# A fused attention and dense kernel: the ordering model's times, held loads, the early output by PE transposes and the band added in PSUM are changed together

## The chip, the cores and the metric

The kernel runs on one core of one Trainium2 chip. The metric is the device time of one execution in microseconds (us); smaller is better. Most executions of a kernel lie within a few us of each other. A run at a lower granted TensorE clock, or over 1.5% above the fastest of its kernel, counts as slow and stays out of the comparisons. Kernels are compared through their ratio to the kernel before, measured in the same rounds.

Names of engines: PE is TensorE, DVE is VectorE, ACT is ScalarE, POOL is GpSimd, SP issues DMAs. A line number such as L626 is a line of the kernel in question, so the same piece of code has different numbers in different kernels.

## The reference, cut to what matters

```python
# q, k, v: 8 batches x 8 heads x 576 tokens x 64
q_d, k_d, v_d = mean over groups of 4 tokens            # 144 pooled tokens
out_up    = repeat(softmax(q_d @ k_d.T / 8) @ v_d, 4)    # pooled attention, each row for 4 tokens
mask      = abs(i - j) < 4                               # a band
out_local = softmax(where(mask, q @ k.T / 8, -1e9)) @ v
x = (out_up + out_local) as [4608 tokens, 512]
h = x @ w_in                                             # [4608, 2048]
return (h - tanh(h)) @ w_out                             # [4608, 512]
```

## The kernel before: the parts that matter

The program is recorded first and ordered afterwards. Every operation is put down with an engine, a duration in ns, the tiles it reads and writes, and its PSUM banks. A list scheduler then runs through a model of the five engines and the DMA queue, decides the order (and, where `choice` offers several engines, which of them does the work), and the instructions are issued in that order. At run time each engine takes its instructions strictly in line. A wrong duration gives no wrong result; it gives an order that makes an engine wait behind something that is late.

```python
class Program:
    LAT = {"PE": 270, "ACT": 150, "DVE": 110, "POOL": 150, "SP": 50, "DMA": 2200}
    ...
    def op(self, eng, ns, fn, reads=(), writes=(), pri=0, slack=0, fill=(), drain=()): ...
    def choice(self, alternatives, ...): ...
    def dma(self, eng, ns, fn, cost, piece, src=(), dst=(), ...): ...
    def order(self): ...        # the list scheduler
```

There are 32 pairs of heads, four for each batch. Dense work on 512 tokens may start when the pairs of their batches have written `xT`. All but the first four pairs run beside dense matmuls. One pair, cut:

```python
        # p >= 12: qr transposed by DMA, then put in place by ACT; before that, PE transposes
        if p >= T_DMA:
            P.dma("SP", 1740, lambda: nc.sync.dma_start_transpose(
                out=qT[s], in_=qr[s].rearrange("p a c -> p (a c)")), 1300, 72, ...)
            op("ACT", 1250, lambda: A.copy(...), reads=[("qT", s)], writes=[("qk", s, 0), ("qk", s, 5)])
        # ... scores s1 and s2 on PE into PSUM t1, t2; then exp, then (p >= 4) the band as a product
        op("ACT", 960, lambda: A.activation(out=e1, in_=two(t1)[:, :, 0:480], func=AF.Exp, scale=SCALE),
           drain=[t1], writes=[("E", e, 0)], pri=pri)
        if p >= NP:
            op("DVE", 950, lambda: V.tensor_tensor(
                out=e1, in0=e1,
                in1=mask[:, 0:480].unsqueeze(1).to_broadcast([128, 2, 480]),
                op=ALU.mult), reads=["mask"], writes=[("E", e, 0)], pri=pri)
        # ... the same for e2v; value product `outs` on PE; reciprocal and ln on DVE
        def back():              # p < 12: out of ln into xT's layout, pooled rows expanded 4 times
            for half in range(2):
                T.matmul(two(tb)[:, half, 0:288], ln[s][:, 5, :], up[:, 288 * half:288 * half + 288],
                         start=True, stop=False)
            T.matmul(two(tb)[:, 1, 224:288], ln[s][0:16, 6, :], up[0:16, 0:64], start=False, stop=False)
            for t in range(NT):
                ...              # 6 matmuls against the identity, added in the same banks
        if p >= X_DMA:           # p >= 12: DMA transpose of ln, then the join
            P.dma("SP", 1350, lambda: nc.sync.dma_start_transpose(...), 1000, 72, ...)
            P.choice([("DVE", 1900, lambda: join(V)), ("POOL", 1400, lambda: join(GP))],
                     reads=[("lT", s)], writes=[("x", b, j)], pri=pri)
            return
        op("PE", 450 * cold, back, ...)
        P.choice([("DVE", 720, lambda: V.tensor_copy(out=xs, in_=two(tb)[:, :, 0:288])), ("ACT", 680, ...)], ...)
```

And a dense block: `mm1` (four matmuls into one bank, tanh on ACT into `u`, subtraction on DVE into `gT`) and `mm2` (sixteen matmuls into one bank, copy on ACT into `y`, store).

The softmax here doesn't subtract the row's maximum and nothing guards it: scores larger than these inputs give would overflow.

Of the kernel before, what the change touches and what calls it, by code (L numbers as in the profile page):

```python
# [9 lines left out]
BF16 = mybir.dt.bfloat16  # L10
AF = mybir.ActivationFunctionType
ALU = mybir.AluOpType
# [11 lines left out]
class Program:  # L24

    LAT = {"PE": 270, "ACT": 150, "DVE": 110, "POOL": 150, "SP": 50, "DMA": 2200}
    RING = 230

    def __init__(self):
        self.ops = []  # L30
        self.alternatives = {}
        self.slack = []
        self.soon = set()
        self.goal = set()
        self.ring = {}
        self.rings = {}
        self.touch = []
        self.use = []
        self.toks = []
        self.cap = {}  # L40
        self.last_write = {}
        self.readers = {}
# [66 lines left out]
    def order(self):  # L109
# [56 lines left out]
        for i in range(n):  # L166
            if left[i] == 0:
                make_ready(i)
        for step in range(n):
            best = None  # L170
            for eng, cand in ready.items():
                if not cand:
                    continue
                now = max(free.get(eng, 0.0), min(at[i] for i in cand))
                if eng == "PE":
# [5 lines left out]
                elif eng == "DMA":  # L181
                    pick = min((turn.get(self.ring[i][0], -1), start[self.ring[i][1]], i)
                               for i in cand if at[i] <= now)[2]
                else:
                    pick = min((self.ops[i][4], i) for i in cand if at[i] <= now)[1]
# [12 lines left out]
            end = now + self.ops[i][1]  # L198
            want = [t for t in self.use[i] if t.first == i]
# [57 lines left out]
def kernel(  # L257
# [41 lines left out]
    mask = fixed("mask", [128, 576], BF16)  # L299
# [19 lines left out]
    up = lT[1].rearrange("p n c -> p (n c)")[:, 0:S]  # L319
    r = fixed("r", [128, 2, 7], FP32, 2)  # L320
    ln = fixed("ln", [128, 7, 128], BF16, 2)
# [31 lines left out]
    def c_up():  # L353

        GP.memset(up, 1.0)
        GP.affine_select(out=up, in_=up, compare_op=ALU.is_ge, fill=0.0,
                         base=0, pattern=[[1, S]], channel_multiplier=-4)
        GP.affine_select(out=up, in_=up, compare_op=ALU.is_ge, fill=0.0,
                         base=3, pattern=[[-1, S]], channel_multiplier=4)

# [8 lines left out]
    def c_mask():  # L369

        GP.memset(mask, 1.0)
        m4 = mask[:, 0:480].rearrange("p (t c) -> p t c", c=QW)
        for part, pat in ((m4, [[0, 4], [1, QW]]),
                          (mask[:, 480:576], [[1, 96]])):
            neg = [[-s, n] for s, n in pat]
            GP.affine_select(
                out=part, in_=part, compare_op=ALU.is_ge, fill=0.0,
                base=-1, pattern=neg, channel_multiplier=1)
            GP.affine_select(
                out=part, in_=part, compare_op=ALU.is_ge, fill=0.0,  # L380
                base=7, pattern=pat, channel_multiplier=-1)
        GP.affine_select(
            out=mask[:, 0:QW], in_=mask[:, 0:QW], compare_op=ALU.is_ge,
            fill=0.0, base=-4, pattern=[[0, QW]], channel_multiplier=1)
        GP.affine_select(
            out=mask[:, 480:576], in_=mask[:, 480:576], compare_op=ALU.is_ge,
            fill=0.0, base=99, pattern=[[0, 96]], channel_multiplier=-1)
# [6 lines left out]
    def load_qk(p):  # L394

        b, h0, s = p // NP, 2 * (p % NP), p % NQKN
        for i, src in enumerate((q, k)):
# [6 lines left out]
            load(600, issue, [("qkn", s, i)], T_QK, 380, -30, 8, (), eng)  # L404

    def load_v(p):
# [3 lines left out]
        for i in range(2):  # L410
# [21 lines left out]
            load(620, issue, [("vst", s, i)], T_V, 100, -30, 40)  # L432
# [24 lines left out]
    def load_v4(p):  # L457
# [8 lines left out]
        load(520, issue, [("v4", s)], 900, 184, -30, 18)  # L466

    def pool_v4(p):
# [9 lines left out]
        op("POOL", 1150, a1, reads=[("v4", s)], writes=["v2"], pri=10 * p - 12)  # L478
        op("POOL", 750, a2, reads=["v2"], writes=[("vp", s)], pri=10 * p - 12)

    def pool_v(hb):
# [15 lines left out]
        op("ACT", 590, lambda: A.copy(  # L497
# [5 lines left out]
    def attention(p):  # L503
# [10 lines left out]
        if p >= NEARLY:  # L514
            op("POOL", 1300, lambda: GP.tensor_copy(  # L515
# [14 lines left out]
        if p >= T_DMA:  # L530
            P.dma("SP", 1740, lambda: nc.sync.dma_start_transpose(
                out=qT[s], in_=qr[s].rearrange("p a c -> p (a c)")), 1300, 72,
                  src=[("qr", s, 0), ("qr", s, 1)], dst=[("qT", s)], pri=-50, lead=500)
            op("ACT", 1250, lambda: A.copy(  # L534
# [3 lines left out]
        else:  # L538
            for a0, a1, tn, cn in ((0, 5, 290, 740), (5, 9, 230, 620)):
# [10 lines left out]
                def copy(fn, a0=a0, a1=a1, b16=b16):  # L550
# [5 lines left out]
                          ("DVE", cn, lambda copy=copy: copy(V.tensor_copy))][:1 + (p < NP)],  # L556
# [10 lines left out]
        def add2(eng):  # L567
            with nc.allow_low_precision("pooled q and k"):
                eng.tensor_tensor(out=qkd[s][:, 0:G],  # L569
                                  in0=half[:, :, 0, :],  # L570
                                  in1=half[:, :, 1, :], op=ALU.add)
        P.choice([(name, n1, lambda eng=eng: add1(eng)) for name, n1, _, eng in adders],
# [41 lines left out]
        if new:  # L614
            op("PE", 620, s12, slack=late, reads=qks + [("qkd", s)], fill=[t1, t2], pri=pri)
        else:
            op("PE", 420 * cold + 250 * (p < NP), s1, slack=late,
               reads=qks + ["bias"] * (p < NP), fill=[t1], pri=pri)
# [3 lines left out]
        op("ACT", 960, lambda: A.activation(  # L622
            out=e1, in_=two(t1)[:, :, 0:480], func=AF.Exp, scale=SCALE),
           drain=[t1], writes=[("E", e, 0)], pri=pri)
        if p >= NP:
            op("DVE", 950, lambda: V.tensor_tensor(  # L626
                out=e1, in0=e1,
                in1=mask[:, 0:480].unsqueeze(1).to_broadcast([128, 2, 480]),
                op=ALU.mult), reads=["mask"], writes=[("E", e, 0)], pri=pri)
        yield  # L630
        if not new:
            op("PE", 380 * cold + 100 * (p < NP), s2, slack=late, reads=qks + [("qkd", s)],
               fill=[t2], pri=pri)
        op("ACT", 310, lambda: A.activation(  # L634
            out=e2v, in_=two(t2)[:, :, 0:96], func=AF.Exp, scale=SCALE),
           drain=[t2], writes=[("E", e, 1)], pri=pri)
        op("ACT", 650, lambda: A.activation(  # L637
            out=e3, in_=two(t2)[:, :, 96:384], func=AF.Exp, scale=SCALE / 16.0),
           drain=[t2], writes=[("E", e, 2)], pri=pri)
        if p >= NP:  # L640
            op("DVE", 450, lambda: V.tensor_tensor(  # L641
                out=e2v, in0=e2v,
                in1=mask[:, 480:576].unsqueeze(1).to_broadcast([128, 2, 96]),
                op=ALU.mult), reads=["mask"], writes=[("E", e, 1)], pri=pri)
# [25 lines left out]
        op("DVE", 200, lambda: V.reciprocal(out=r[s], in_=blocks()[:, :, :, 64]),  # L670
           drain=[to], writes=[("r", s)], pri=pri)
        op("DVE", 1060, lambda: V.tensor_tensor(  # L672
# [6 lines left out]
        tb = P.psum(2, kind)  # L679

        def back():
            for half in range(2):
                T.matmul(two(tb)[:, half, 0:288], ln[s][:, 5, :], up[:, 288 * half:288 * half + 288],
                         start=True, stop=False)
            T.matmul(two(tb)[:, 1, 224:288], ln[s][0:16, 6, :], up[0:16, 0:64],
                     start=False, stop=False)
            for t in range(NT):
                q0, q1 = QW * t, QW * t + NQ[t]
                for half in range(2):
                    c0, c1 = max(q0, 288 * half), min(q1, 288 * half + 288)  # L690
                    if c0 < c1:
                        T.matmul(two(tb)[:, half, c0 - 288 * half:c1 - 288 * half],  # L692
                                 ln[s][0:NQ[t], t, :], ident[0:NQ[t], c0 - q0:c1 - q0],
                                 start=False, stop=(t == (2, NT - 1)[half]))
        if p >= X_DMA:
            P.dma("SP", 1350, lambda: nc.sync.dma_start_transpose(
                out=lT[s], in_=ln[s].rearrange("p n c -> p (n c)")), 1000, 72,
# [3 lines left out]
            def join(eng):  # L701
# [12 lines left out]
            P.choice([("DVE", 1900, lambda: join(V)), ("POOL", 1400, lambda: join(GP))],  # L714
                     reads=[("lT", s)], writes=[("x", b, j)], pri=pri)
            return
        op("PE", 450 * cold, back, slack=late, reads=[("ln", s), ("lT", 1), "ident"],
           fill=[tb], pri=pri)
        xs = xT[j][:, b * S:(b + 1) * S].rearrange("p (n c) -> p n c", n=2)
        P.choice([("DVE", 720, lambda: V.tensor_copy(out=xs, in_=two(tb)[:, :, 0:288])),  # L720
                  ("ACT", 680, lambda: A.copy(out=xs, in_=two(tb)[:, :, 0:288]))],
                 drain=[tb], writes=[("x", b, j)], pri=pri)
# [4 lines left out]
    def mm1(kb, fc):  # L727
# [14 lines left out]
        op("ACT", 590, lambda: A.activation(  # L742
            out=u[us], in_=one(tok), func=AF.Tanh),
           drain=[tok], writes=[("u", us)], pri=DPRI)
        op("DVE", 670, lambda: V.tensor_tensor(  # L745
# [6 lines left out]
    def mm2(kb, i):  # L752
        ts, part, g = i // 4, i % 4, kb % 2
        if part == 0:
            ycur[0] = P.psum(1, "d")
        tok = ycur[0]

        def mm(e):
            for fc in range(4 * part + 2 * e, 4 * part + 2 * e + 2):
                T.matmul(one(tok), gT[g][:, fc, ts * 128:ts * 128 + 128],  # L760
                         w_out_sb[:, fc, :],
                         start=(fc == 0), stop=(fc == N_FF - 1))
        for e in range(2):
            op("PE", 432, lambda e=e: mm(e),
               reads=[("w_out", part, c) for c in range(4)] +
               [("gT", g, fc) for fc in range(4 * part, 4 * part + 4)],
               fill=[tok], pri=5000)
        if part == 3:
            ys = yn[0] % 3
            yn[0] += 1  # L770
            op("ACT", 590, lambda: A.copy(out=y[ys], in_=one(tok)),  # L771
               drain=[tok], writes=[("y", ys)], pri=DPRI)
            r0 = kb * 512 + ts * 128
            P.dma("SP", 530, lambda: nc.sync.dma_start(
                out=out[r0:r0 + 128, :], in_=y[ys]), 700, 344, src=[("y", ys)], pri=DPRI)

    def dense(kb):
# [13 lines left out]
        for i in range(16):  # L791
            if kb < NBLK:
# [4 lines left out]
    M2_FIRST, T_DMA, X_DMA, NEW, LATE = 16, 12, 12, 12, 0  # L797
    DPRI = -1
    T_QK, T_V, T_W, W_PRI, NEARLY = 800, 1000, 2850, 32, NP
    CAST_V = [[("POOL", 820, GP.tensor_copy), ("ACT", 640, A.copy)],  # L800
              [("POOL", 820, GP.tensor_copy)]]
    any3 = [("DVE", 700, V.tensor_copy), ("ACT", 650, A.copy),
            ("POOL", 750, GP.tensor_copy)]
# [141 lines left out]
```

## Time and profile before

| | before |
|---|---|
| time, 3 runs | 336.77 us median (335.35 to 337.07) |
| profiled execution | 331.7 us, span 329.7 us, granted clock 1.0 |
| first dense matmul (head) | 25.4 us |
| from there to the end of the last matmul (stretch) | 299.9 us |
| after the last matmul (tail) | 4.4 us |

The page of the kernel before, its parts 1 and 2: busy us, share of the span and instructions of each engine; and the busy share of the DMA engines in 40 slices of the span, in tenths:

```profile
PE 314.8 (95%) x2420; PEld 158.8 (48%) x2461; DVE 214.0 (65%) x330; ACT 202.4 (61%) x334; POOL 177.3 (54%) x211
DMA  7999999999999999999999999972320011000121
```

PE is busy nearly always, so PE's list of work and PE's waits decide. DMA is full until about 214 us, so what arrives when is decided by the order of the queue.

The engines' busy time between 120 and 185 us, kernel before. After the length of the stretch come busy us (and instructions) of PE, weight loads, DVE, ACT and POOL, the granted clock, the DMA share and GB/s:

```profile
120.00:185.00 65.00, 61.26 (x514) 30.79 (x521) 57.14 (x73) 44.82 (x72) 57.05 (x62) 1.00 1.11 246
```

DVE and POOL are at 88% of this stretch, and PE, which should be the limit, is at 94%.

Whom PE waited for, kernel before: us in total, number of waits, the longest:

```profile
PE bank L650 <- DVE E L641: 2.0, 2, 1.4
...
PE bank L650 <- DVE E L626: 0.5, 1, 0.5
PE bank L650 <- DVE gT L745: 0.4, 1, 0.4
```

L650 is the value product; L626 and L641 are the two mask products. The groups of DVE instructions show why those are late. After the bar come busy us and the mean ns of one, then the idle time before them:

```profile
L672 DVE TENSOR_TENSOR ln<-bank,r 128x896 bf16<-128x896 f32 x32 | 34.7, 1087 | 0.9
L626 DVE TENSOR_TENSOR E<-E,mask 128x960 bf16<-128x960 bf16 x28 | 32.3, 1154 | 11.5 <-ACT E L622 11.4
L641 DVE TENSOR_TENSOR E<-E,mask 128x192 bf16<-128x192 bf16 x28 | 16.1, 576 | 0.7 <-ACT E L634 0.7
L703 DVE TENSOR_TENSOR xT<-lT 128x480 bf16<-128x480 bf16 x9 | 12.3, 1366 | 1.4 <-DMA lT<-ln 1.4
```

The means hide a spread. L626 takes 0.641 us at best, 0.896 in the median, 3.479 at worst; L672, which reads PSUM, stays between 1.027 and 1.093.

```profile
124.79 0.67 POOL L569 TENSOR_TENSOR qkd<-half 128x288 bf16<-128x288 f32 x1
125.43 1.00 POOL L703 TENSOR_TENSOR xT<-lT 128x480 bf16<-128x480 bf16 x1
126.40 0.34 POOL L709 TENSOR_TENSOR xT<-lT 128x96 bf16<-128x96 bf16 x1
126.69 1.14 POOL L515 CAST qr<-qkn 128x1152 bf16<-128x1152 f32 x1
```

The multiply, which takes 0.64 us at best, ended only 0.5 us after four POOL instructions that followed each other without a gap.

### The profile page before, as it was taken

What the parts mean: (1) busy time and instruction counts of PE and PEld (TensorE: products, weight loads), DVE (VectorE), ACT (ScalarE), POOL (GpSimd) and SP (SyncE); (2) the same over time, 40 slices, a digit from 0 to 9 for tenths busy, and PEclk for the clock granted to TensorE, in tenths of its full rate; (3) what the DMA queues carried; (4) which work ended last, traced back from release to release, by engine and by line L of the source; (5) the groups of instructions that cost most, each with busy time, mean ns of one, the idle gap of its engine ahead of it and who ended that gap; (6) DMA issues with size and microseconds to landing.
All of it is one profiled execution on the core that took longest, in us unless ns stands there. A gap on an engine that the chain in (4) does not pass through costs nothing.

```text
span 329.7 us, 6505 instructions
## 1 busy us (share of the span) xinstructions
PE 314.8 (95%) x2420; PEld 158.8 (48%) x2461; DVE 214.0 (65%) x330; ACT 202.4 (61%) x334; POOL 177.3 (54%) x211
## 2 busy tenths in 40 slices
PE   7989999999999999999899899999999999999994
PEld 2654555665444544444444445444444444444441
DVE  4767864479966969888989869757754433444300
ACT  4968864588778866687867375868543444344311
POOL 8664547959667698869899848787310000000000
PEclk9999999999999999999999999999999999999999
DMA  7999999999999999999999999972320011000121
GB/s 233 288 235 228 241 229 218 316 278 234 284 224 254 226 208 264 252 253 269 206 257 247 251 238 276 212 172 61 91 60 34 32 52 45 32 32 32 43 86 65
DMA packets 108862, 59.80 MB, mean 181 GB/s; under 512 B 86174, under 2 KB 96030, under 8 KB 108830
## 3 DMA queue, kind: packets, MB, share of 16 engines
q1 hardware_dynamic: 104318, 54.60, 71.0%
q0 software_dynamic: 4224, 4.19, 7.7%
q10 hardware_dynamic: 288, 0.59, 0.6%
q8 instruction: 19, 0.31, 0.4%
q14 instruction: 13, 0.11, 0.1%
HBM read 43.64 MB, written 9.44 MB: 161 GB/s over the span
## 4 chain that ended last, share of the span: by engine, by line
PE 76%; DVE 12%; DMA 3%; ACT 3%; POOL 2%; issue 2%; ACTq 0%; DVEq 0%; POOLq 0%
PE bank L760 32%; PE bank L734 32%; DMA lT<-ln 3%; DVE E L626 3%; PE bank L650 3%; PE bank L584 3%; DVE ln L672 3%; DVE gT L745 2%; PE bank L657 2%; DVE E L641 2%; DVE xT L709 1%; ACT E L622 1%; PE bank L692 1%; DVE xT L703 1%; PE bank L547 1%
## 5 line engine op out<-in xcount | busy, mean ns | idle before, releaser
L734 PE MATMUL bank<-xT,w_in_sb 128*128 128x512 bf16 x557 | 143.7, 379 | 1.4 <-DVE gT L745 0.3
L760 PE MATMUL bank<-w_out_sb,gT 128*128 128x512 bf16 x555 | 141.6, 379 | 1.5 <-issue 0.6
L745 DVE TENSOR_TENSOR gT<-bank,u 128x512 bf16<-128x512 f32 x144 | 97.3, 685 | 61.4 <-ACT u L742 60.9
L742 ACT ACTIVATE u<-bank 128x512 f32<-128x512 f32 x144 | 86.0, 598 | 76.7 <-PE bank L734 73.6
L760 PEld LDWEIGHTS <-gT 128*128 128x128 bf16 x576 | 53.9, 98 | 62.0
L734 PEld LDWEIGHTS <-w_in_sb 128*128 128x128 bf16 x576 | 53.9, 98 | 61.9 <-issue 0.5
L564 POOL TENSOR_TENSOR half<-qk 128x576 f32<-128x576 bf16 x28 | 32.1, 1146 | 20.7 <-ACT qk L551 12.3
L626 DVE TENSOR_TENSOR E<-E,mask 128x960 bf16<-128x960 bf16 x28 | 32.3, 1154 | 11.5 <-ACT E L622 11.4
L622 ACT ACTIVATE E<-bank 128x960 bf16<-128x960 f32 x32 | 31.2, 974 | 12.3 <-PE bank L584 12.2
L515 POOL CAST qr<-qkn 128x1152 bf16<-128x1152 f32 x28 | 32.7, 1169 | 8.0 <-DMA qT<-qr 5.5
L672 DVE TENSOR_TENSOR ln<-bank,r 128x896 bf16<-128x896 f32 x32 | 34.7, 1087 | 0.9
L771 ACT COPY y<-bank 128x512 f32<-128x512 f32 x36 | 21.1, 586 | 19.7 <-PE bank L760 18.3
L451 POOL CAST vw<-vst 128x640 bf16<-128x640 f32 x31 | 25.4, 824 | 7.5 <-DMA vst<-in_v_dram 7.5
L472 POOL TENSOR_TENSOR v<-v 72x512 f32<-72x512 f32 x20 | 25.4, 1272 | 1.2 <-DMA v<-in_v_dram 0.4
L534 ACT COPY qk<-qT 128x1152 bf16<-128x1152 bf16 x20 | 24.1, 1205 | 0.6 <-DMA qT<-qr 0.6
L650 PE MATMUL bank<-vw,E 128*128 128x65 bf16 x320 | 20.1, 194 | 3.1 <-DVE E L641 2.0
L569 POOL TENSOR_TENSOR qkd<-half 128x288 bf16<-128x288 f32 x29 | 21.0, 725 | 1.7 <-DVE r L670 0.8
L476 POOL TENSOR_TENSOR vp<-v 72x256 bf16<-72x256 f32 x20 | 14.6, 730 | 13.1 <-PE bank L657 13.0
L650 PEld LDWEIGHTS <-E 128*128 128x128 bf16 x320 | 16.5, 98 | 10.2 <-DVE E L641 2.5
L637 ACT ACTIVATE E<-bank 128x576 bf16<-128x576 f32 x32 | 21.1, 660 | 0.0
L703 POOL TENSOR_TENSOR xT<-lT 128x480 bf16<-128x480 bf16 x11 | 11.2, 1017 | 14.4 <-DMA lT<-ln 14.3
L641 DVE TENSOR_TENSOR E<-E,mask 128x192 bf16<-128x192 bf16 x28 | 16.1, 576 | 0.7 <-ACT E L634 0.7
(75 smaller groups left out, 225.7 us busy)
## 6 DMA issues: line engine op xcount, KB each, us to landing
vst<-in_v_dram SPq DMA_DIRECT2D x62, 160.0 KB, 5.2
qkn<-in_q_dram SPq DMA_DIRECT2D x32, 288.0 KB, 5.4
out_dram<-y SPq DMA_DIRECT2D x36, 256.0 KB, 4.7
qkn<-in_k_dram SPq DMA_DIRECT2D x30, 288.0 KB, 5.7
v<-in_v_dram SPq DMA_DIRECT2D x20, 288.0 KB
w_in_sb<-in_moe_w_in_dram POOLq DMA_DIRECT2D x4, 512.0 KB, 11.7
w_out_sb<-in_moe_w_out_dram POOLq DMA_DIRECT2D x4, 512.0 KB, 10.3
qkn<-in_k_dram ACTq DMA_DIRECT2D x2, 288.0 KB, 3.3
```

The costliest lines, as they stand in the source:

```text
L451: P.choice([(eng, ns, lambda fn=fn: fn(out=vw[w][:, 2 * jj:2 * jj + 2, :, 0:64], in_=vst[s])) for eng, ns, fn in CAST_V[p >= NEARLY]], rea ...
L472: GP.tensor_tensor(out=v2, in0=v4[s][:, :, :, 0:128], in1=v4[s][:, :, :, 128:256], op=ALU.add)
L515: op("POOL", 1300, lambda: GP.tensor_copy(out=qr[s].rearrange("p a (h d) -> p h a d", h=2), in_=qkn[sn].rearrange("p h (a d) -> p h a d", ...
L564: eng.tensor_tensor(out=half, in0=four[:, :, 0:2, :], in1=four[:, :, 2:4, :], op=ALU.add)
L622: op("ACT", 960, lambda: A.activation(out=e1, in_=two(t1)[:, :, 0:480], func=AF.Exp, scale=SCALE), drain=[t1], writes=[("E", e, 0)], pri=pri)
L626: op("DVE", 950, lambda: V.tensor_tensor(out=e1, in0=e1, in1=mask[:, 0:480].unsqueeze(1).to_broadcast([128, 2, 480]), op=ALU.mult), reads= ...
L650: T.matmul(two(to)[:, hh, 65 * t:65 * t + 65], E[e][:, c:c + 128], vw[w][:, 2 * jj + hh, t, :], start=True, stop=True)
L672: op("DVE", 1060, lambda: V.tensor_tensor(out=ln[s].rearrange("p n (h d) -> p h n d", d=D), in0=blocks()[:, :, :, 0:64], in1=r[s].unsqueez ...
L734: T.matmul(one(tok), w_in_sb[:, dc, fc * 128:(fc + 1) * 128], xT[dc][:, kb * 512:kb * 512 + 512], start=(dc == 0), stop=(dc == N_DC - 1))
L742: op("ACT", 590, lambda: A.activation(out=u[us], in_=one(tok), func=AF.Tanh), drain=[tok], writes=[("u", us)], pri=DPRI)
L745: op("DVE", 670, lambda: V.tensor_tensor(out=gT[g][:, fc, :], in0=one(tok), in1=u[us], op=ALU.subtract), drain=[tok], reads=[("u", us)], w ...
L760: T.matmul(one(tok), gT[g][:, fc, ts * 128:ts * 128 + 128], w_out_sb[:, fc, :], start=(fc == 0), stop=(fc == N_FF - 1))
```

## The change: its intent, and the diff

Four things are changed together.

1. The ordering model gets longer DMA times (a transpose of q and k 1684 instead of 1300 ns, of the output 1317 instead of 1000), shorter engine times, a rule for DVE and POOL additions that exclude each other, and `mm2` banks of its own. From pair 17 on, loads of q and k wait for the DMA transpose of the pair five before.
2. Work is placed differently: joins on POOL only, v casts also on ACT, scores as one block from pair 8 (before: 12), the last 128 output rows in two halves.
3. The output of the first 12 pairs goes through seven PE transposes into one bank; the pooled rows are added by DVE.
4. The band is added in PSUM, as -32768, before exp, instead of multiplied after exp.

The diff, cut (`...` marks cuts; changes of a mere duration are left out except a few):

```diff
-    LAT = {"PE": 270, "ACT": 150, "DVE": 110, "POOL": 150, "SP": 50, "DMA": 2200}
+    LAT = {"PE": 235, "ACT": 145, "DVE": 110, "POOL": 140, "SP": 50, "DMA": 2000}
...
+            if eng == "POOL" or eng == "DVE" and i in self.port:
+                port = end
...
-            P.dma("SP", 1740, lambda: nc.sync.dma_start_transpose(
-                out=qT[s], in_=qr[s].rearrange("p a c -> p (a c)")), 1300, 72,
+            P.dma("SP", 1340, lambda: nc.sync.dma_start_transpose(
+                out=qT[s], in_=qr[s].rearrange("p a c -> p (a c)")), 1684, 92,
...
-        if new:
-            op("PE", 620, s12, ...)
+        if p >= MERGE:
+            op("PE", 590, s12, ...)
...
+        def band(tok, lo, hi):
+            part = two(tok)[:, :, 0:hi - lo]
+            V.tensor_tensor(out=part, in0=part, in1=bias[:, lo:hi].unsqueeze(1)
+                            .to_broadcast([128, 2, hi - lo]), op=ALU.add)
+        if p >= NP:
+            op("DVE", 1080, lambda: band(t1, 0, 480), reads=["bias"], fill=[t1], pri=pri)
         op("ACT", ..., lambda: A.activation(out=e1, in_=two(t1)[:, :, 0:480], func=AF.Exp, scale=SCALE), ...)
-        if p >= NP:
-            op("DVE", 950, lambda: V.tensor_tensor(out=e1, in0=e1, in1=mask[:, 0:480]..., op=ALU.mult), ...)
...
-        tb = P.psum(2, kind)
+        tb = P.psum(1, kind)
         def back():
-            for half in range(2):
-                T.matmul(two(tb)[:, half, 0:288], ln[s][:, 5, :], up[:, 288 * half:288 * half + 288], ...)
-            ...
+            for t in range(7):
+                q0, n = (QW * t, NQ[t]) if t < NT else (S + 128 * (t - NT), (128, 16)[t - NT])
+                T.transpose(flat()[:, q0:q0 + n], ln[s][0:n, t, :], ident[0:n, 0:n])
...
-            P.choice([("DVE", 1900, lambda: join(V)), ("POOL", 1400, lambda: join(GP))],
+            P.choice([("POOL", 1310, lambda: join(GP))],
...
+        P.choice([("DVE", 130, lambda: V.tensor_copy(out=od[s], in_=flat()[:, S:S + G])), ("ACT", 170, ...)], ...)
+        op("DVE", 610, lambda: V.tensor_tensor(
+            out=xT[j][...], in0=flat()[:, 0:S]..., in1=od[s].unsqueeze(2).to_broadcast([128, G, 4]), op=ALU.add), ...)
...
+        split = kb == NBLK - 1 and ts == 3      # the last output rows: two banks of 256 columns
...
-    CAST_V = [[("POOL", 820, GP.tensor_copy), ("ACT", 640, A.copy)],
-              [("POOL", 820, GP.tensor_copy)]]
+    CAST_V = [[("POOL", 770, GP.tensor_copy), ("ACT", 620, A.copy)],
+              [("POOL", 770, GP.tensor_copy), ("ACT", 620, A.copy)]]
...
-            load_qk(nl[0])
+            t = nl[0] - BACK                    # BACK = 5
+            load_qk(nl[0], [("qT", t % 2)] if t >= T_DMA else ())
...
-    P.cap = {"b": 6, "d": 4}
+    P.cap = {"b": 6, "d": 4, "y": 3}
```

## The prediction

> **What bounds the kernel now.** TensorE. The busy table gives PE 314.8 of 329.7 us (95%), VectorE 65%, ScalarE 61%, GpSimd 54%; PEclk is full throughout. The chain of waits has three parts. (1) A head of 25.4 us until the first dense matmul (L734): an attention prologue over all engines, with mask, ident, group and expansion matrix made in turn on POOL, and a last pair whose loads land at about 13 us. (2) A PE stretch from 25.4 to 325.3 us: 1152 dense matmuls at a pitch of 0.216 us are 249 us, so attention's matmuls, changes of operand and stalls take some 51 us. (3) A tail of 4.4 us: y copy (0.59 us), then the store.
> The timeline shows true PE stalls of about 4.5 us in part 2. The largest (0.66, 0.61, 0.82, 1.4 us, between 127 and 184 us) are in the value product (L650), waiting for VectorE: mask multiply L641 or a late gT. The mask multiply (L626) takes 0.64 us at best, 1.15 on average, 3.48 at worst. The Trainium skill, "SBUF — State Buffer", section "SBUF: two separate sides", says a VectorE operation with two SBUF inputs and a GpSimd operation reading SBUF exclude each other for the whole instruction; this spread agrees, while PSUM readers (L672: 1.03 to 1.09 us) hardly vary.
>
> **What the change does, costed.**
> - Output by PE transposes for the first 12 pairs: L683+L685+L692 cost 0.85 us of PE a pair inside the dense stretch (6.8 us for 8). Seven transposes at the 0.056 us pitch of L547 are 0.4 us. Critical: -3.4 us.
> - Scores issued as one block for pairs 8 to 11: -0.8 us of PE.
> - Band added in PSUM before exp: two VectorE operations of, estimated from L745 and L672, 1.1 and 0.3 us, nearly constant, instead of 1.15 and 0.58 with long outliers. The value product then waits for ScalarE only. All joins go to POOL (9 x 2.26 us leave VectorE, 9 x 1.48 us reach POOL); 19 v casts leave POOL for ScalarE. Of 4.5 us of stalls I expect 3 to go.
> - Longer DMA times and loads held back: DMA share is above 1.0 from 25 to 185 us, so the bytes get no cheaper; only transposes should wait less. A guard against new stalls.
> - Head: the expansion matrix (1.9 us of POOL) and the bias operation go, ident comes first. But pairs 2 and 3 wait for loads, and the output gets a copy plus an add on VectorE. -0.6 us.
> - Tail: last output in two halves, smaller copy and store: -0.5 us.
>
> Sum -8.3 us; I give 1 us back for new waits, since PSUM is held longer by the band add and x now comes from POOL alone.
>
> **Prediction.** 329.2 us from 336.77 (-2.2%), range 326 to 333.5. Faster by over 2%: 0.56; within 2%: 0.42; slower: 0.02.
>
> **What would show it.** Output transposes near 0.43 us a pair on PE; first dense matmul at 24.5 to 25.2 us; the band add near 1.1 us with little spread, VectorE busy from 214 to about 185 us; no wait of L650 on VectorE's mask; POOL about 175 us; PE stalls in the dense stretch under 2 us; tail under 4.1 us. Wrong if PE stalls do not shrink, or the dense start does not move.
>
> **What would make it wrong.** The order is fixed in advance: if DMA transposes land later than planned, PE waits in line at scores (L584), or dense blocks wait for POOL's xT. If the head is bound only by loads, its gain vanishes and the result stays just within 2%. If the stalls vanish entirely and the head shrinks by 2 us, it goes to 326.

## More of the kernel before

The worst L626, in the order of time of DVE and then of POOL (start us, length us):

```profile
124.86 3.48 DVE L626 TENSOR_TENSOR E<-E,mask 128x960 bf16<-128x960 bf16 x1
```

## The result, and the profile after

| | before | after |
|---|---|---|
| time, 4 runs each | 336.21 us median (335.35 to 337.07) | 326.65 us median (325.31 to 327.17) |
| ratio | | 0.971, 95% interval 0.967 to 0.975: faster |
| profiled execution | 331.7 us, span 329.7 us | 327.17 us, span 325.3 us |
| head, stretch, tail | 25.4, 299.9, 4.4 us | 25.0, 296.8, 3.4 us |

A ratio is, to within 0.001, the mean time of one kernel's fast runs over that of the other's of the same rounds, so it is not quite the ratio of the medians.

The two traces differ by 4.4 us (head -0.4, stretch -3.1, tail -0.9), the timed runs by 9.6 us. The trace of before is of a quick execution: of the 53 other timed runs of before (without one slow profiled run) only one was below 331.7 us. So part of the timed gain is not seen in the traces.

The page after, the same lines:

```profile
PE 311.2 (96%) x2410; PEld 159.9 (49%) x2450; DVE 193.4 (59%) x322; ACT 207.4 (64%) x353; POOL 168.4 (52%) x209
DMA  7999999799974999999999999999711300000021
```

DVE lost 21 us. DMA has a gap between about 90 and 106 us (its share between 98 and 106 us is 0.49), where loads are held back; u_dma below, which holds none back, has no such gap. The windows view after, 120 to 185 us:

```profile
120.00:185.00 65.00, 64.29 (x494) 32.08 (x501) 40.70 (x64) 46.73 (x78) 46.26 (x54) 1.00 1.09 246
```

DVE fell from 57.1 to 40.7 us in this stretch, POOL from 57.1 to 46.3, and PE rose to 99%. The groups after, of the band and the join:

```profile
L626 DVE TENSOR_TENSOR bank<-bank,bias 128x960 f32<-128x960 f32 x28 | 32.4, 1159 | 19.3 <-PE bank L586 16.2 <-ACT vw L452 3.1
L626 DVE TENSOR_TENSOR bank<-bank,bias 128x192 f32<-128x192 f32 x28 | 10.0, 356 | 1.9 <-PE bank L608 1.9
L696 POOL TENSOR_TENSOR xT<-lT 128x480 bf16<-128x480 bf16 x20 | 20.2, 1009 | 16.4 <-DMA lT<-ln 16.4
```

The large band addition is no quicker on average than the product was (1.159 against 1.154 us), but its slowest is 1.167 us. Whom PE waited for after:

```profile
PE bank L764 <- DMA w_out_sb<-in_moe_w_out_dram: 2.0, 1, 2.0
...
PE bank L731 <- DVE gT L742: 0.7, 1, 0.7
```

The waits for the mask are gone and a new one has come: 2.0 us for the last quarter of `w_out`. In sum, PE's waits in the stretch (those over 0.15 us) were 4.3 us before and are 4.2 us after, so in these two traces they hardly shrank. The stretch is shorter because the rest of it, PE's work and its smaller steps, fell from 295.6 to 292.6 us. In order of time on PE after (start us, length us; x is the number of matmuls merged in the line), both the transposes and the wait:

```profile
55.31 0.59 PE L687 MATMUL bank<-ident,ln 120*128 120x120 bf16 x7
55.84 0.40 PE L548 MATMUL bank<-ident,qr 128*128 128x128 bf16 x4
56.07 1.46 PE L764 MATMUL bank<-w_out_sb,gT 128*128 128x512 bf16 x6
57.37 0.59 PE L687 MATMUL bank<-ident,ln 120*128 120x120 bf16 x7
59.98 0.38 PE L764 MATMUL bank<-w_out_sb,gT 128*128 128x512 bf16 x1 [2.02 <-DMA w_out_sb<-in_moe_w_out_dram]
```

From one start to the next, seven transposes take 55.84 - 55.31 = 0.53 us. The quarter of `w_out` lands at 59.94 us; before, it landed at 58.79 us and PE did not wait for it.

### The profile page after: what moved, and what is told of

Same layout as the page of the kernel before. It is cut to its first block, busy times and chain, and to the rows that moved or that the text cites. A ratio compares the mean times of both kernels' runs of the same rounds, so it can differ in the third digit from the quotient of the medians.

```text
span 325.3 us, 6523 instructions
## 1 busy us (share of the span) xinstructions
PE 311.2 (96%) x2410; PEld 159.9 (49%) x2450; DVE 193.4 (59%) x322; ACT 207.4 (64%) x353; POOL 168.4 (52%) x209
## 4 chain that ended last, share of the span: by engine, by line
PE 82%; DVE 5%; DMA 4%; issue 2%; SPq 2%; POOL 2%; ACT 2%; ACTq 0%; POOLq 0%; DVEq 0%
PE bank L764 37%; PE bank L731 35%; DMA w_out_sb<-in_moe_w_out_dram 3%; PE bank L586 3%; PE bank L650 3%; PE bank L657 2%; DMA vst<-in_v_dram 2%; DVE gT L742 1%; DVE bank L626 1%; SPq L402 1%; PE bank L608 1%; ACT u L739 1%; DVE xT L715 1%; PE bank L548 1%; PE bank L687 1%
## 5 line engine op out<-in xcount | busy, mean ns | idle before, releaser
L764 PE MATMUL bank<-w_out_sb,gT 128*128 128x512 bf16 (+1 forms) x575 | 135.3, 374 | 3.0 <-DMA w_out_sb<-in_moe_w_out_dram 2.0
L731 PE MATMUL bank<-xT,w_in_sb 128*128 128x512 bf16 x554 | 135.4, 380 | 2.4 <-issue 0.8
L764 PEld LDWEIGHTS <-gT 128*128 128x128 bf16 x592 | 56.0, 98 | 63.6 <-issue 2.2
L565 POOL TENSOR_TENSOR half<-qk 128x576 f32<-128x576 bf16 x29 | 33.2, 1145 | 53.6 <-ACT qk L552 26.0
L626 DVE TENSOR_TENSOR bank<-bank,bias 128x960 f32<-128x960 f32 (+1 forms) x56 | 41.4, 757 | 21.2 <-PE bank L586 16.2
L776 ACT COPY y<-bank 128x512 f32<-128x512 f32 (+1 forms) x37 | 21.3, 575 | 32.4 <-PE bank L764 31.5
L696 POOL TENSOR_TENSOR xT<-lT 128x480 bf16<-128x480 bf16 x20 | 20.2, 1009 | 16.4 <-DMA lT<-ln 16.4
L670 DVE RECIPROCAL r<-bank 128x14 f32<-128x14 f32 x32 | 7.7, 240 | 24.5 <-PE bank L657 21.4
L570 POOL TENSOR_TENSOR qkd<-half 128x288 bf16<-128x288 f32 x30 | 20.0, 665 | 2.4 <-DVE half L565 1.4
L586 PEld LDWEIGHTS <-qk 64*128 64x128 bf16 x320 | 9.3, 94 | 13.5 <-issue 9.3
```

The lines of the kernel that those rows point to most:

```text
L565: eng.tensor_tensor(out=half, in0=four[:, :, 0:2, :], in1=four[:, :, 2:4, :], op=ALU.add)
L626: V.tensor_tensor(out=part, in0=part, in1=bias[:, lo:hi].unsqueeze(1) .to_broadcast([128, 2, hi - lo]), op=ALU.add)
L731: T.matmul(one(tok), w_in_sb[:, dc, fc * 128:(fc + 1) * 128], xT[dc][:, kb * 512:kb * 512 + 512], start=(dc == 0), stop=(dc == N_DC - 1))
L764: T.matmul(one(tok)[:, 0:n], gT[g][:, fc, ts * 128:ts * 128 + 128], w_out_sb[:, fc, cols:cols + n], start=(fc == 0), stop=(fc == N_FF - 1))
```

## The experiments

Twelve runs in four calls, each against the kernel before. All outputs are right. The calls ran on different chips (numbered 3, 0, 7 and 2), so a difference between two kernels of one call counts for more than one across calls. Several runs undo or do one part; as the order is made anew for each, every one of them is a new plan of the whole program, not the old plan with a piece exchanged.

| call | kernel | this, median us | before, median us | ratio (95%) |
|---|---|---|---|---|
| 1 | before again | 333.91 | 333.33 | 1.001 (0.996 to 1.005) |
| 1 | after again | 328.39 | 333.33 | 0.985 (0.981 to 0.988) |
| 1 | output transposes alone | 332.24 | 333.33 | 0.998 (0.994 to 1.001) |
| 1 | band in PSUM alone | 335.30 | 333.33 | 1.004 (1.000 to 1.008) |
| 2 | order and placement alone | 328.87 | 333.92 | 0.986 (0.983 to 0.990) |
| 2 | both pieces, old order | 338.40 | 333.92 | 1.015 (1.011 to 1.019) |
| 2 | after without transposes | 327.02 | 333.92 | 0.981 (0.977 to 0.984) |
| 2 | after without band in PSUM | 328.76 | 333.92 | 0.987 (0.982 to 0.991) |
| 3 | after, w_out's last parts later | 328.50 | 333.49 | 0.983 (0.979 to 0.987) |
| 3 | after, old joins and casts | 331.35 | 333.49 | 0.994 (0.990 to 0.998) |
| 3 | after, old DMA times, no hold | 332.38 | 333.49 | 0.997 (0.994 to 1.000) |
| 4 | after, w_out's last quarter earlier | 326.84 | 334.92 | 0.977 (0.972 to 0.982) |

### c_before2 and c_after2: both kernels again

No edit.

> The kernel before, unchanged, against itself. The timed gain (336.2 to 326.7 us, 9.6 us) is twice the gain between the two traces (329.7 to 325.3 us, 4.4 us). Theory 1: the trace of before is of an unusually quick execution; its waits for DMA vary from execution to execution, so a second trace shows a span of 333 to 335 us, with more than 4.5 us of PE stalls in the dense stretch. Theory 2: before is always about 5 us quicker when profiled; the span is 329 to 330.5 us again. Ratio of the timed runs 0.997 to 1.003 under both.

> The changed kernel, unchanged, for its spread and a second trace. Ratio 0.967 to 0.976 again. Theory 1 (before's DMA waits vary, the change's do not): timed runs within 2 us of each other, span 323.5 to 325.5 us, and again one PE stall of about 2 us at 57.8 us for the last quarter of w_out. Rival: the w_out stall was an accident of that execution and is below 0.5 us.

Measured: 1.001 and 0.985. The profiled execution of before fell in the slow state (408.4 us, granted clock 0.755), so theory 1 and theory 2 of the missing trace time stay undecided. The second set says something else of weight: in this set the change gives 1.5%, not 2.9%, and the two intervals do not meet. Whether the chip makes the difference is not known. Its five timed runs lay within 2.4 us. The w_out wait came again (1.8 us at 61 us, 2.2 in two waits), and the head was 26.7 us instead of 25.0, for a reason that the order of time on PE of this run shows:

```profile
24.38 0.61 PE L917 MATMUL bank<-lT 128*128 128x512 bf16 x2
26.66 1.69 PE L731 MATMUL bank<-xT,w_in_sb 128*128 128x512 bf16 x7 [1.68 <-DMA w_in_sb<-in_moe_w_in_dram]
```

The first quarter of `w_in` landed at 26.61 us here and at 24.25 us in the first trace. So in this trace a load bounds the head; in the first, the load had landed 0.8 us before the first dense matmul.

### a_out: the output transposes alone

The kernel before with the new `back`, the copy of the pooled columns and the addition on DVE; `od` lies in `lT[1]`, free until pair 12; `mask` keeps its own room.

```diff
+    od = [lT[1].rearrange("p n c -> p (n c)")[:, G * i:G * i + G] for i in range(2)]
-        tb = P.psum(2, kind)
+        tb = P.psum(1, kind)
...      # back, copy and addition as in the change; c_up and its operation removed
```

> Only the output of the first 12 pairs by PE transposes, in the kernel before. Theory A (parts add up on PE): 8 pairs in the dense stretch save 0.43 us of PE each, -3.4 us, and the head up to -0.6 us: ratio 0.987 to 0.990. Rival B (the order as a whole makes the gain; PE time saved in one place is lost in waits that move): ratio 0.994 to 1.003.

Measured: 0.998, rival B. The transposes do take 0.52 us a pair on PE. But DVE's busy time rose from 214.0 to 220.3 us, and PE waited 2.3 us for gT in the dense stretch where it had waited 0.7. Its waits there in sum are no longer, though (4.0 against 4.3 us), so that these waits took the saved time is not shown.

### a_band: the band in PSUM alone

```diff
-    op("POOL", 2700, c_mask, ...)            # and the DVE operation that made bias from mask
+    op("POOL", 2700, c_bias, writes=["bias"], pri=-97)
...      # band() before each exp, as in the change; both mask products removed
```

> Only the band added in PSUM before exp, in the kernel before (order made with its old times). Theory A: the value product no longer waits for VectorE's mask, PE stalls between 120 and 185 us fall by 2 to 3 us, ratio 0.990 to 0.994; the band add takes 1.1 us with little spread and VectorE's busy time falls by about 10 us. Rival B: the stalls return as other waits (PSUM held longer, joins on VectorE), ratio 0.996 to 1.005.

Measured: 1.004, rival B. The addition was as constant as expected (1.155 to 1.167 us) and DVE's busy time fell by 9.5 us, so this half of the mechanism is shown; it brought no time. The profiled execution is a slow one and its waits are not compared.

### a_order and u_order: the order and placement without the two pieces, and the reverse

`a_order` is the change without items 3 and 4. `u_order` is the kernel before with items 3 and 4 and nothing else. (The exps' durations in the ordering model go with item 4.)

> Everything but the two rewritten pieces of arithmetic, in the kernel before: new durations in the ordering model, loads held back, joins on POOL only, v casts also on ScalarE, output banks of their own, scores as one block from pair 8, last output halved; output still by expansion matmul, band still multiplied after exp. Theory C (the two pieces alone gave 0.998 and 1.004 because VectorE, which makes gT, stayed as full as before; what frees it is the order part, by moving the joins): ratio 0.988 to 0.993. Theory A (parts add up): the order part must then be worth nearly all of the change, 0.984 to 0.988. Rival D (order part alone is worth nothing, the gain needs all three): 0.996 to 1.004.

> The two rewritten pieces together (PE transposes for the early output, band in PSUM), with the old ordering model, joins and casts as before. Theory C: VectorE is still nearly as full, waits for gT or ln eat the saved PE time: ratio 0.995 to 1.003. Theory A: sum of the parts alone, 1.00. If it is below 0.990 the two pieces needed each other, not the order part.

Measured: 0.986 and 1.015. Order and placement alone give what the full change gave in the call before (0.985). The two pieces of arithmetic, in a plan made with the old times and placement, make the kernel 1.5% slower, worse than either alone and worse than any of the theories said. PE's waits in u_order:

```profile
PE bank L720 <- DVE ln L661: 2.0, 2, 1.4
PE bank L720 <- DVE xT L685: 1.7, 1, 1.7
PE bank L676 <- DVE ln L661: 1.7, 3, 0.9
...
PE bank L720 <- ACT E L619: 1.5, 1, 1.5
```

Behind them is ACT. What the readers and writers of the DMA-transposed tile qT waited for between 100 and 230 us in u_order (us, times); the same view of a_order shows no wait of ACT at all for this tile:

```profile
its engine sat idle before it (us, times) until:
  DMA qT<-qr: 9.5, 6
```

ACT stands in line for 9.5 us with exps and tanhs behind it, because the transposes are not there when their turn comes; two waits of PE for an exp (0.8 us, ended at 164.8; 1.5 us, ended at 169.5) begin 1.8 and 0.6 us after ACT's waits of 3.4 and 1.9 us for this tile. That ACT is behind the waits for DVE too is argued, not followed link by link. Nor do the old DMA times by themselves make this wait: in the kernel before, planned with the same times, ACT waited 0.6 us for this tile (shown under u_dma), and 4.4 us in a_out. Another part of the trace's length is a granted clock of one half for 3.4 us from 197.5 us on, some 1.7 us (an estimate: half of 3.4); but u_order's one timed run at clock 1.0 took 337.3 us, still 1.1% above before.

### u_out and u_band: the changed kernel without one piece

`u_out` puts the expansion matmuls back, `u_band` the mask products; both keep the new order.

```diff
+    op("POOL", 1700, c_up, writes=[("lT", 1)], pri=-50)      # u_out, with the old back and copy
+    op("POOL", 2700, c_mask, writes=["mask"], pri=-97)       # u_band, with bias from mask on DVE
```

> The changed kernel with the early output by expansion matmul again. Theory C: with VectorE freed, PE time counts in full; 8 pairs lose 0.43 us each in the dense stretch and the head up to 0.5 us: 3.4 to 4 us slower than the changed kernel, so 0.996 to 0.999 of before if the changed kernel is at 0.985. Rival D': the output pieces are worth nothing here either, 0.983 to 0.988.

> The changed kernel with the band as a multiplication after exp again. Theory C: VectorE gets 10 us back and POOL, now with all joins, blocks the multiplies for up to 3 us at a time; value products wait for the mask again, 2 to 3 us of PE stalls: ratio 0.991 to 0.995. Rival: VectorE has room, the outliers do not reach PE: 0.983 to 0.988.

Measured: 0.981 and 0.987. Rival D' holds for the output (the ratio is even a little below its range): without transposes the kernel is not 3.4 us slower; in its call it is the quickest. The order of time on PE in u_out shows what an expansion costs and where the time went:

```profile
57.84 0.41 PE L691 MATMUL bank<-lT,ln 128*128 128x288 bf16 x2
58.18 0.20 PE L693 MATMUL bank<-lT,ln 16*128 16x64 bf16 x1
58.31 0.43 PE L700 MATMUL bank<-ident,ln 120*128 120x120 bf16 x6
58.58 0.59 PE L775 MATMUL bank<-w_out_sb,gT 128*128 128x512 bf16 x2
59.64 1.67 PE L775 MATMUL bank<-w_out_sb,gT 128*128 128x512 bf16 x7 [0.46 <-DMA w_out_sb<-in_moe_w_out_dram]
```

An expansion takes 58.58 - 57.84 = 0.74 us, so a transpose saves 0.22 us a pair, 1.8 us for 8 pairs, and half of these pairs lie before the w_out wait. With the expansions PE reaches w_out later and waits 0.46 instead of 2.0 us; but its dense stretch also begins 1.0 us later (26.0 against 25.0 us), so not all of that is the expansions' doing. For the band, u_band lies in the range of the rival and outside that of theory C. Its slowest mask product is 2.15 us instead of 3.48, and PE waited 0.96 us in all for the mask: the new order had already taken most of these waits away. One comparison within this call goes the other way: a_order has neither piece and u_out has the band in PSUM alone, and u_out is 1.9 us quicker in the median, with no run of one in the range of the other (326.5 to 328.0 against 328.1 to 330.3 us). So in the new order the band in PSUM seems to be worth some 0.6%, and the transposes (u_band against a_order) nothing.

### x_late: the parts of mm2 that need w_out's last quarter later

```diff
-            for i in range(M2_FIRST):
+            for i in sorted(range(M2_FIRST), key=lambda i: (i // 8, i % 4 == 3, i)):
                 mm2(kb, i)
```

(and a bank for each token tile, `ycur[ts]`.)

> The changed kernel, with the first dense output block in another order: for each pair of token tiles the parts that need the last quarter of w_out come after the other six. Theory W (the PE time that the early transposes save before 60 us is eaten by the wait for the last quarter of w_out, 2.0 us in both traces of the changed kernel): the wait falls below 0.3 us, the dense stretch from 296.4 to 294 to 295 us, about 2 us faster than the changed kernel: ratio 0.976 to 0.981. Rival: another wait takes its place (gT from VectorE at 73 us, xT of batch 1), ratio 0.982 to 0.987.

Measured: 0.983; the rival's number, but not its reason. The wait did not go away: it was 2.9 us. The order had no room left to gain: in both kernels PE has done the 36 matmuls that three output banks allow without the last quarter (36 records in the second trace of after and in x_late) before it waits. The windows view of this run, 60 to 66 us, shows what such a wait can set off (the columns are as above; the clock is the number after POOL):

```profile
60.00:66.00 6.00, 5.72 (x26) 2.19 (x26) 0.74 (x1) 1.17 (x2) 1.72 (x2) 0.50 0.41 106
```

The granted clock fell to one half at 59.35 us and came back at 66.18 us, so the matmuls from 60.28 to 66.18 us ran at half speed and some 3 us were lost once more (an estimate: half of 5.9 us). In the two traces of the changed kernel the wait, 2.0 and 1.8 us long, set off nothing. The clock bears on x_late's ratio too: its two timed runs at clock 1.0 took 325.9 and 326.3 us, 0.977 of before's mean, and the four at 0.990 to 0.995 took 328.3 to 330.0 us. So the test of theory W is not clean.

### u_join and u_dma: which half of the order part

`u_join` lets the planner choose DVE for joins and POOL alone for late v casts, as before; `u_dma` takes the old DMA times and drops the hold.

```diff
 # u_join
-            P.choice([("POOL", 1310, lambda: join(GP))],
+            P.choice([("DVE", 1900, lambda: join(V)), ("POOL", 1310, lambda: join(GP))],
-              [("POOL", 770, GP.tensor_copy), ("ACT", 620, A.copy)]]
+              [("POOL", 770, GP.tensor_copy)]]
 # u_dma
-    LAT = {..., "DMA": 2000}
+    LAT = {..., "DMA": 2200}
-    T_QK, T_V, T_W, W_PRI, NEARLY = (760, 864), (850, 939), 3000, 32, NP
+    T_QK, T_V, T_W, W_PRI, NEARLY = (800, 800), (1000, 1000), 2850, 32, NP
-            load_qk(nl[0], [("qT", t % 2)] if t >= T_DMA else ())
+            load_qk(nl[0])
 ...     # transposes 1300 and 1000 ns again, v4 load 900
```

> The changed kernel with the joins allowed on VectorE again (10 of 20 go there) and the v casts after pair 4 on POOL only, all other things as changed. Theory C (moving joins and casts is what makes the order part worth 1.4%): VectorE's stretch of 120 to 185 us is full again, waits of PE for gT, ln or xT of 2 us or more, ratio 0.991 to 1.000. Rival P (the durations and the holding back of loads in the plan matter, not who does the joins): 0.982 to 0.988.

> The changed kernel with the DMA times of the kernel before in the ordering model and no holding back of loads. Theory P (realistic DMA times and the hold are what makes the order part): transposes land later than planned, PE waits in line at scores or value products by 3 us or more between 100 and 220 us: ratio 0.992 to 1.003. Theory C: little changes, 0.982 to 0.988.

Measured: 0.994 and 0.997, beside 0.983 for x_late, which stands in for the changed kernel and differs from it by an order that did not remove the wait. Both halves count: 1.1% for placement, 1.4% for DMA times and hold. The two add up to more than the 1.7% of x_late, so they are not terms of a sum. Theory C and theory P each named one of two causes. In u_join, DVE is busy 49.6 us between 120 and 185 us (after: 40.7), and PE waited 2.9 us for w_out, 1.4 for an exp and 1.4 for gT in the whole stretch. But between 120 and 185 us, where theory C looked for the loss, PE did not wait at all:

```profile
120.00:185.00 65.00, 65.00 (x514) 32.38 (x513) 49.63 (x74) 44.69 (x72) 51.30 (x57) 1.00 1.15 247
```

Its trace is of the slowest of its six runs, with a granted clock of one half for 3.4 us at 197 us. So the placement counts by the ratio; how it costs the time is not shown.

In u_dma, the view of qT between 100 and 230 us reads:

```profile
its engine sat idle before it (us, times) until:
  DMA qT<-qr: 10.1, 5
```

that of the changed kernel:

```profile
its engine sat idle before it (us, times) until:
  PE bank L586: 0.7, 1
```

and that of the kernel before, which has the old DMA times and no hold as u_dma does:

```profile
its engine sat idle before it (us, times) until:
  DMA qT<-qr: 0.6, 1
```

ACT stood 10.1 us in line for transposes that came later than their turn; in the two traces of the changed kernel it stood 0 and 0.5 us. So the old times without the hold bring the wait only together with other parts of the change, for in the kernel before it is short. PE then waited for exps:

```profile
PE bank L586 <- ACT E L630: 1.1, 1, 1.1
...
PE bank L731 <- ACT E L630: 1.0, 1, 1.0
```

The first of these began 1.5 us after a 3.2 us wait of ACT for qT; the second, at 154 us, follows none. PE's waits in the stretch sum to 5.9 us, against 4.2 and 3.2 us in the two traces of the changed kernel, while the stretch is 4.3 and 4.8 us longer. So part of the loss is seen as waits, and for the rest the cause is open.

### x_early: the last quarter of w_out loaded with the third

```diff
-        if 0 <= nl[0] - NP - 1 < 4:
+        if 0 <= nl[0] - NP - 1 < 3:
             load_w(moe_w_out, w_out_sb, "w_out", nl[0] - NP - 1, ("vst", (nl[0] - 1) % NVST, 1))
+        if nl[0] - NP - 1 == 2:
+            load_w(moe_w_out, w_out_sb, "w_out", 3, ("vst", (nl[0] - 1) % NVST, 1))
```

> The changed kernel with the last quarter of w_out loaded together with the third (behind the v load of the same pair), so it is issued at about 44 us instead of 51. x_late did not remove the wait: the plan already put off the parts that need this quarter, as far as its three output banks allow; only an earlier load can. Theory W: the wait of 2 us at 58 us is gone (below 0.3 us), the stretch is 294 to 295 us, ratio 0.976 to 0.982, the best of the study. Rival: the earlier 512 KB delay the loads and transposes of the next pairs and another wait takes its place, ratio 0.983 to 0.988.

Measured: 0.977, inside the range of theory W. The wait for w_out is gone from the trace. But the stretch there (in the second-slowest of its six runs) is 298.0 us, not 294 to 295, and the waits that its PE shows are many small ones:

```profile
PE bank L608 <- POOL qkd L570: 1.2, 2, 0.9
PE bank L731 <- DVE gT L742: 1.1, 2, 0.6
...
PE bank L731 <- ACT y L776: 0.7, 1, 0.7
```

So the rival is right about the waits and theory W about the ratio. As the changed kernel measured 0.971 and 0.985 in two sets, a better version than the change is not shown.

## Why the prediction was right or wrong, point by point

The time and the direction were right: 329.2 us was predicted, with 326 to 333.5 as range, and 326.65 us was measured. The sum that led there was wrong in its largest term, so that it came near is in part luck: 3.4 us were booked for transposes that brought none that the runs show, nothing was booked for the DMA times and the hold, and the gain itself was 2.9% in one set and 1.5% in the next.

- "Output by PE transposes ... Critical: -3.4 us." This step failed. The PE time a pair was sized from 0.85 against 0.4 us; it is 0.74 against 0.53. The 0.85 came from a sum over a trace in which 40 of 1152 dense matmul records were missing, and their time had fallen to the neighbours. The 0.4 us assumed seven transposes at one pitch: five of them keep about 0.05 us from start to start, but in the trace of after the 128-row block takes 0.152 and the 16-row block 0.111. That leaves 1.8 us for 8 pairs. Even this did not come through: alone, the piece gave 0.998; undone, it cost nothing (0.981), and there the wait for w_out is 1.5 us shorter.
- "A guard against new stalls" for the DMA times and the hold. This failed too: it is a part of the gain that counts, 1.4%, while order and placement as a whole give 0.986 without either piece of arithmetic. The reading that DMA bytes get no cheaper was right: 246 GB/s between 120 and 185 us in both kernels. What was missed is that a transpose that comes later than its turn stops ACT, which works in line: 10.1 us in u_dma, 9.5 in u_order, 0 and 0.5 after. The kernel before, with the old times, shows only 0.6 us, so the wait that the new times and the hold guard against seems to be one that the other parts of the change bring.
- Stalls, "I expect 3 to go". The waits for the mask and its neighbours, 2.9 us in three lines before, went. A wait of 2.0 us for w_out came, which the prediction did not foresee; it named xT and scores as places for new waits. In sum the waits in the stretch were 4.2 us in the first trace of after and 3.2 in the second, from 4.3, where under 2 had been predicted: by the prediction's own test ("Wrong if PE stalls do not shrink") this part is wrong. What shrank instead is the rest of the stretch, by 3.0 us; a_order, without either piece, has 1.5 us of that. The band in PSUM was named as the cause, but u_band shows that the new order removed most of these waits by itself; what the band may be worth in that order is the 0.6% between a_order and u_out. The SBUF reading held: products over two SBUF operands spread from 0.64 to 3.48 us, the addition in PSUM from 1.154 to 1.167.
- VectorE "from 214 to about 185 us": 193.4 us; the output's addition (12 x 0.75 us) had been left out. "POOL about 175 us": 168.4.
- Scores as one block, -0.8 us: not measured by itself; it is a candidate for the 1.5 us of a_order.
- Head, -0.6 us: -0.4 in one trace, +1.2 in the other, where the load of w_in came later. Tail, -0.5 us: -0.9 us (4.4 to 3.4 us in both traces).

What stays open: the first traces show a gain of 4.4 us, while the timed gain was 9.6 us in the first set and 4.9 us in the second, with only one fast trace of before. How much of the difference between the sets is the chip, how much arrival of loads, and how much is a clock that falls after a wait, no run here tells. Nor were the shorter engine times, the exclusion rule, the banks of `mm2` and the one-block scores tried one by one.

## What to carry to other kernels

When a planner fixes the order, its durations are part of the kernel: two pieces of arithmetic that each saved engine time made the kernel 1.5% slower in the old plan and cost nothing in the new one. Before counting a saving on the busiest engine as time, ask what it waits for next; here part of the time saved before 60 us only brought PE earlier to a load that had not landed. Judge each part by a run in which the rest of the plan is made for it, and read the ratio in more than one set of runs.

## What the Trainium skill lacked or had wrong

- "SBUF — State Buffer", section "SBUF: two separate sides": it says that the first of a VectorE operation with two SBUF inputs and a GpSimd operation that reads SBUF holds the shared ports for its whole instruction and the other blocks. The trace agrees, and adds what the page lacks, a case of several in a row: a product that takes 0.64 us at best took 3.48 us beside four GpSimd instructions without a gap, and ended 0.5 us after the last; the large addition with one operand in PSUM never exceeded 1.167 us.
- "TensorE: Matmul & The Clock Gate", section "Back-to-back issue gap": it gives about 131 ns a matmul as sustained spacing for 512 columns in a stream of weight loads and matmuls. Here such a stream, at full granted clock, keeps 216 ns in every trace, which is what the page's formula for an isolated gap gives.
- The same page, section "What's actually happening": it gives the fall to half clock after at least one idle window of about 3.4 us. In x_late the granted clock was halved at 59.35 us, 1.95 us after the last matmul ended, in an idle time of 2.88 us in all, and stayed so for 6.83 us; the matmuls then started 0.427 us apart instead of 0.216. In u_order and u_join it was halved for 3.41 us from 197 us on, with no PE wait longer than 1.71 and 1.44 us just before. A wait of 2.02 us in after set off nothing, so no length of wait decides it alone.
- The same page, section "Part 4: PE-mode transpose": it gives the length of one transpose, about 275 ns in a kernel, and no spacing. Here one takes 0.219 us, and 128x128 transposes in a row start 0.056 us apart; in a row with blocks of other heights, the 128-row block before the 16-row block takes 0.152 us and the 16-row block 0.111 us.
- None of the pages that were read says by how much a DMA transpose that shares the queue with loads can come late; in u_dma its reader stood idle for 10.1 us in five waits, up to 3.3 us in one.
